# Sliding-window attention on one core: scores in quarters of the TensorE array, then used as weights over rows of values, gated values and ones

## The chip, the cores and the metric

The kernel runs on one core of a Trainium2 chip. A core has TensorE (PE, matmuls; its weight loads are shown apart as PEld), VectorE (DVE), ScalarE (ACT), GpSimd (POOL) and SyncE (SP), each with an instruction queue of its own, and 16 DMA engines that all queues share. The metric is the device time of one execution in microseconds (us). Everything is float32.

## The reference

Attention with a causal window of 64 keys over 8 batches, 8 heads, 576 positions and head size 64; its output, 512 wide for each of the 4608 tokens, goes into a mixture of 8 experts. A token takes its own best expert or that of the token before it, as a local gate says.

```python
scores = scale * np.matmul(q, k.transpose(0, 1, 3, 2))
rel = pos[:, None] - pos[None, :]
mask = (rel >= 0) & (rel < window)            # window = 64
...
attn = attn / (np.sum(attn, axis=-1, keepdims=True) + 1e-09)
x = np.matmul(attn, v)                         # then (B, S, H*D)
...
logits = np.einsum('bsd,de->bse', x, w_gate)
local_gate = 1.0 / (1.0 + np.exp(-np.einsum('bsd,de->bse', x, w_local).squeeze(-1)))
...
            e = fresh_e if s == 0 or local_gate[b, s] < 0.5 else prev_e
            h = np.maximum(x[b, s] @ w1[e], 0.0)
            out[b, s] = p[e] * (h @ w2[e])
```

## The kernel before

The program has three stages: `attention`, which writes the attended rows to `xs` in DRAM and the nine gate sums of each token (8 experts and the local gate) to `lt`; `route`, which sorts tokens by expert; and `experts`, which gathers the rows and runs the two matmuls of each expert. A `flag` behind attention says whether the sums of exponentials were in a safe range (line 110 writes `bad`); if not, a careful version would run, which it doesn't on these inputs. The routing's instructions stand behind the flag.

Attention runs over 9 chunks of 512 tokens (`sc`), and in each over 4 pairs of heads (`hp`). One pair of heads of one chunk is a unit. Keys and queries come in blocks of 64, and a query block needs its own key block and the one before. The steps of a unit:

- `scores` (lines 170 to 185): for each of 8 key blocks one matmul whose weights, `kt`, are a 128x128 block-diagonal matrix made on the host: the first head's 64 keys in one corner, the second head's in the other, zeros elsewhere. It is multiplied with 128 queries (the block itself and the next). The result, keys in rows, goes to `sp`; ScalarE makes exponentials of it (line 183, 1024 wide), VectorE multiplies with the mask (line 184).
- `values` (lines 187 to 206): the same with block-diagonal values `vt`, nine matmuls that leave `xp`, features in rows, tokens in columns (one of them takes the last key block of the chunk before). GpSimd adds up the exponentials that belong to one query into `t` (lines 199 to 204), and ScalarE copies `xp` to `xt`.

Once a chunk, `gates` multiplies `xt` with the gate weights and `t` with a selector of ones: eight matmuls of 512 columns, each 32 outputs wide in one of four column strips of the array. `rows` turns the gate sums (4 transposes) and `xt` (16 transposes) back to tokens in rows, divides by the sums (`r`), adds up the gates into `lt`, and stores 128 rows at a time to `xs` through GpSimd's queue (line 244). The two buffers of `x` come free when such a store has landed. `load` brings `qt` (1152 KB), `kt` and `vt` (2048 KB each) for a chunk through SP's queue, two chunks ahead at the start, one chunk ahead later. The order of instructions on all engines is the scheduler's.

Of the kernel before, what the change touches and what calls it, by code (L numbers as in the profile page):

```python
# [8 lines left out]
F32 = mybir.dt.float32  # L9
# [9 lines left out]
P = 128  # L19
# [4 lines left out]
WIN = 64  # L24
# [22 lines left out]
GW = 32  # L47


@with_exitstack  # L50
def kernel(
# [5 lines left out]
    k2: bass.AP,  # L57
    v2: bass.AP,
# [28 lines left out]
    attention(tc, q, k2, v2, xs, lt, ok, wg2s, ident)  # L87
# [26 lines left out]
def attention(ctx, tc, q, k2, v2, xs, lt, ok, wg2, ident):  # L114
# [22 lines left out]
    col = cp.tile([P, 2 * KB, WIN], I32, name="col")  # L137
    nc.gpsimd.iota(col, pattern=[[0, 2 * KB], [1, WIN]], base=0, channel_multiplier=0)
    colf = cp.tile([P, 2 * KB, WIN], F32, name="colf")
    nc.vector.tensor_copy(colf, col)  # L140
    mask = cp.tile([P, 2 * KB, 2 * WIN], F32, name="mask")
    nc.vector.tensor_scalar(mask[:, :, :WIN], colf, rowf, None, Alu.is_ge)
    nc.vector.tensor_scalar(mask[:, :, WIN:], colf, rowf, None, Alu.is_lt)
    nc.vector.memset(mask[:, KB - 1, WIN:], 0.0)


    sel = cp.tile([P, GW], F32, name="sel")
    nc.vector.memset(sel, 0.0)
    for i in range(2):
        nc.vector.memset(sel[i * WIN:(i + 1) * WIN, 2 * (E + 1) + i:2 * (E + 1) + i + 1], 1.0)  # L150

    allsum = cp.tile([P, NSC, 4, H], F32, name="allsum")

    qts, kts, vts = {}, {}, {}

    def load(sc):
        t0 = sc * SC
        n = min(SC + WIN, N - t0)
        qt = qts[sc] = qp.tile([P, HP, SC + WIN], F32, name="qt")
        kt = kts[sc] = qp.tile([P, HP, KB, P], F32, name="kt")  # L160
        vt = vts[sc] = qp.tile([P, HP, KB, P], F32, name="vt", bufs=3)
        step = 1 if sc == 0 else HP
        for i in range(0, HP, step):
            h = slice(i, i + step)
            nc.sync.dma_start(out=qt[:, h, :n], in_=q[:, h, t0:t0 + n])
            nc.sync.dma_start(out=kt[:, h], in_=k2[sc, :, h])
            nc.sync.dma_start(out=vt[:, h], in_=v2[sc, :, h])

    last = {}

    def scores(sc, hp):
        qt, kt = qts[sc], kts[sc]
        sp = ps_s.tile([P, KB, 2 * WIN], F32, name="sp")
        for j in range(KB):
            n = 2 * WIN if sc * KB + j + 1 < N // WIN else WIN
            nc.tensor.matmul(sp[:, j, :n], lhsT=kt[:, hp, j, :],  # L176
                             rhs=qt[:, hp, j * WIN:j * WIN + n], start=True, stop=True)
        p = pp.tile([P, KB, 2 * WIN], F32, name="p")
        m = (KB - sc if sc else KB)
        full = KB if (sc + 1) * SC < N else KB - 1  # L180
        for a, b, w in ((0, full, 2 * WIN), (full, KB, WIN)):
            if a < b:
                nc.scalar.activation(p[:, a:b, :w], sp[:, a:b, :w], Act.Exp, scale=DH ** -0.5)  # L183
                nc.vector.tensor_tensor(p[:, a:b, :w], p[:, a:b, :w], mask[:, m + a:m + b, :w], op=Alu.mult)  # L184
        return p

    def values(sc, hp, p, t, xt):
        vt = vts[sc]
        before = last.get(hp)
        xp = ps_x.tile([P, SC], F32, name="xp")  # L190
        if before is not None:
            nc.tensor.matmul(xp[:, :WIN], lhsT=vts[sc - 1][:, hp, KB - 1, :], rhs=before[:, KB - 1, WIN:],
                             start=True, stop=False, skip_group_check=True)
        for j in range(KB):
            n = 2 * WIN if j + 1 < KB else WIN
            nc.tensor.matmul(xp[:, j * WIN:j * WIN + n], lhsT=vt[:, hp, j, :], rhs=p[:, j, :n],  # L196
                             start=(before is None and j == 0), stop=(j == KB - 1), skip_group_check=True)

        nc.gpsimd.tensor_tensor(t[:, hp, WIN:].rearrange("p (b q) -> p b q", q=WIN), p[:, 1:, :WIN],  # L199
                                p[:, :KB - 1, WIN:], op=Alu.add)  # L200
        if before is not None:
            nc.gpsimd.tensor_tensor(t[:, hp, :WIN], p[:, 0, :WIN], before[:, KB - 1, WIN:], op=Alu.add)
        else:
            nc.gpsimd.tensor_copy(t[:, hp, :WIN], p[:, 0, :WIN])
        nc.scalar.copy(xt[:, hp, :], xp)
        last[hp] = p

    def gates(sc, t, xt):

        gp = ps_x.tile([P, SC], F32, name="gp")  # L210
        for hp in range(HP):
            g = gp[hp * GW:(hp + 1) * GW, :]
            nc.tensor.matmul(g, lhsT=wg2[:, hp, :], rhs=xt[:, hp, :], start=True, stop=False, skip_group_check=True)
        for hp in range(HP):
            g = gp[hp * GW:(hp + 1) * GW, :]
            nc.tensor.matmul(g, lhsT=sel, rhs=t[:, hp, :], start=False, stop=True, skip_group_check=True)
        gs = wk.tile([P, SC], F32, name="gs")
        nc.vector.tensor_copy(gs, gp)
        return gs

    def rows(sc, xt, gs):
        gt = ps_x.tile([P, 4, HP, GW], F32, name="gt")
        for c in range(4):
            nc.tensor.transpose(gt[:, c].rearrange("p h g -> p (h g)"), gs[:, c * P:(c + 1) * P], ident)
        su = allsum[:, sc].rearrange("p c (h j) -> p c h j", j=2)
        nc.vector.tensor_copy(su, gt[:, :, :, 2 * (E + 1):2 * (E + 1) + 2])
        r = wk.tile([P, 4, H], F32, name="r")
        nc.vector.tensor_scalar(r, allsum[:, sc], 1e-9, None, Alu.add)
        nc.vector.reciprocal(r, r)
        for c in range(4):  # L230
            n = sc * 4 + c
            g = wk.tile([P, HP, 2, E + 1], F32, name="g")
            rc = r[:, c, :]
            nc.vector.tensor_tensor(g, gt[:, c, :, :2 * (E + 1)].rearrange("p h (j e) -> p h j e", j=2),
                                    rc.rearrange("p (h j o) -> p h j o", j=2, o=1).to_broadcast([P, HP, 2, E + 1]),
                                    op=Alu.mult)
            nc.vector.tensor_reduce(lt[:, n, :], g.rearrange("p h j e -> p e (h j)"), axis=AX.X, op=Alu.add)
            xr = ps_x.tile([P, H, DH], F32, name="xr")
            for hp in range(HP):
                nc.tensor.transpose(xr[:, 2 * hp:2 * hp + 2, :].rearrange("p h d -> p (h d)"),  # L240
                                    xt[:, hp, c * P:(c + 1) * P], ident)
# [9 lines left out]
    for i, (sc, hp) in enumerate(units):  # L251
        if hp == 0:
            t = wk.tile([P, HP, SC], F32, name="t")
            xt = wk.tile([P, HP, SC], F32, name="xt")
# [515 lines left out]
```

## Time and profile before

| what | us |
|---|---|
| median of 3 runs (883.41 to 887.78) | 885.82 |
| the profiled execution | 886.19 |
| its span, first to last instruction | 883.9 |
| TensorE busy in the span | 802.9 |
| VectorE busy | 194.2 |
| ScalarE busy | 110.8 |
| GpSimd busy | 163.5 |

The page divides the span into 40 equal slices of 22.1 us. The windows, the timeline, the waits and the groups of instructions are answers from the same trace for a stretch or an engine. In a line of the timeline stand the start, the duration, the engine, the line of the program, the operation, what is written and read, the shapes, the count of merged instructions, and in brackets how long the engine had been idle and who released it. A float32 matmul shows as two MATMUL and two LDWEIGHTS instructions (two passes), a transpose as one of each.

### The profile page before, as it was taken

Reading aid. Unit: us, or ns where it says so; the run is one execution under the profiler, and the core shown is the slowest. Engines: PE = TensorE matmul, PEld = TensorE weight load, DVE = VectorE, ACT = ScalarE, POOL = GpSimd, SP = SyncE. Lnnn points to the kernel's source line nnn. Section 1 sums busy time; section 2 is a strip of 40 time slices with the busy share of each in tenths; the row PEclk is TensorE's granted clock in tenths of the full one; section 3 lists DMA queues with packets and bytes.
Section 4 is the critical chain, followed back from the end, with each engine's and each line's share of the span. In section 5 each row is a group of like instructions: output and inputs, shape, how many; then the busy total and the mean of one; then the engine's idle time right before and its main releaser. Section 6 shows DMA issues by size and latency. Waiting matters only on the chain. (4 is left out here: it accounts for less than half of the span.)

```text
span 883.9 us, 10273 instructions
## 1 busy us (share of the span) xinstructions
PE 802.9 (91%) x4279; PEld 596.2 (67%) x4279; DVE 194.2 (22%) x468; ACT 110.8 (13%) x158; POOL 163.5 (18%) x209
## 2 busy tenths in 40 slices
PE   6998888989455599999999999999999999999996
PEld 6787687878143367766676667766777777676864
DVE  3443444454794010000110011000101010101010
ACT  2232222222000000100001000100000101010100
POOL 2433332343102200111110111111111111111000
PEclk9999899899655599999999999999999999999999
DMA  9967766541104995354544545364888888888883
GB/s 342 411 274 292 293 253 237 210 199 67 47 0 187 420 403 202 125 232 147 216 166 185 207 162 217 132 234 144 318 328 328 322 323 324 329 329 318 313 305 122
DMA packets 27147, 213.50 MB, mean 242 GB/s; under 512 B 3821, under 2 KB 3837, under 8 KB 16848
## 3 DMA queue, kind: packets, MB, share of 16 engines
q1 hardware_dynamic: 17472, 182.46, 53.6%
q0 software_dynamic: 9616, 30.24, 8.7%
q8 instruction: 38, 0.62, 0.3%
q14 instruction: 21, 0.17, 0.1%
HBM read 193.81 MB, written 19.92 MB: 242 GB/s over the span
## 5 line engine op out<-in xcount | busy, mean ns | idle before, releaser
L686 PEld LDWEIGHTS hp<-xt,w 128*128 128x128 f32 x1856 | 266.6, 192 | 31.6 <-issue 13.4
L686 PE MATMUL hp<-xt,w 128*128 128x128 f32 (+1 forms) x1856 | 287.2, 316 | 0.0
L698 PE MATMUL yp<-w,h 128*128 128x512 f32 x640 | 279.5, 592 | 0.0
L698 PEld LDWEIGHTS yp<-w,h 128*128 128x128 f32 x640 | 119.5, 190 | 139.3 <-issue 137.0
L690 DVE TENSOR_SCALAR h<-hp 128x512 f32<-128x512 f32 x40 | 27.7, 692 | 522.7 <-issue 401.3
L702 POOL DMA_INDIRECT out_dram<-y,idx x40 | 40.0, 999 | 304.7 <-ACT y L701 291.6
L196 PE MATMUL xp<-p,vt 128*128 128x128 f32 (+1 forms) x576 | 77.6, 290 | 15.8 <-DVE p L184 15.6
L660 POOL DMA_INDIRECT xg<-xs,idx x43 | 42.1, 979 | 258.4 <-PE tp L674 191.4
L196 PEld LDWEIGHTS xp<-p,vt 128*128 128x128 f32 x576 | 73.6, 206 | 17.5 <-DVE p L184 16.3
L176 PE MATMUL sp<-qt,kt 128*128 128x128 f32 x576 | 78.3, 289 | 7.5 <-DMA kt<-in_k_dram 7.5
L176 PEld LDWEIGHTS sp<-qt,kt 128*128 128x128 f32 x576 | 72.6, 202 | 13.7 <-issue 13.7
L701 ACT ACTIVATE y<-yp,pw 128x512 f32<-128x512 f32 x40 | 27.5, 687 | 367.6 <-PE yp L698 357.8
L199 POOL TENSOR_TENSOR t<-p 128x448 f32<-128x448 f32 x36 | 44.9, 1248 | 68.9 <-DVE p L184 68.9
L184 DVE TENSOR_TENSOR p<-p,mask 128x1024 f32<-128x1024 f32 (+2 forms) x40 | 45.0, 1141 | 44.6 <-ACT p L183 44.6
L692 ACT ACTIVATE h<-hp 128x512 f32<-128x512 f32 x40 | 23.9, 597 | 224.1 <-PE hp L686 224.1
L183 ACT ACTIVATE p<-sp 128x1024 f32<-128x1024 f32 (+2 forms) x40 | 36.9, 933 | 91.4 <-PE sp L176 71.3
L674 PE MATMUL tp<-ident,xg 128*128 128x128 f32 x160 | 25.7, 296 | 21.8 <-DMA xg<-xs,idx 21.8
L674 PEld LDWEIGHTS tp<-ident,xg 128*128 128x128 f32 x160 | 20.3, 153 | 24.8 <-issue 21.0
L243 DVE TENSOR_TENSOR x<-xr,r 128x512 f32<-128x512 f32 x36 | 24.7, 685 | 42.2 <-DMA xs<-x 41.2
L244 POOL DMA_DIRECT2D xs<-x x36 | 19.7, 548 | 71.6 <-DVE x L243 37.8
L633 PE MATMUL tab<-colh,rowh 128*128 128x86 f32 x72 | 22.4, 467 | 10.7 <-DVE colh L632 10.7
L240 PE MATMUL xr<-ident,xt 128*128 128x128 f32 x144 | 23.4, 284 | 8.4 <-DVE x L243 8.4
(152 smaller groups left out, 270.9 us busy)
## 6 DMA issues: line engine op xcount, KB each, us to landing
w<-in_w_dram SPq DMA_DIRECT2D x64, 2048.0 KB, 8.2
kt<-in_k_dram SPq DMA_DIRECT2D x8, 2048.0 KB, 11.9
vt<-in_v_dram SPq DMA_DIRECT2D x8, 2048.0 KB, 13.7
xs<-x POOLq DMA_DIRECT2D x36, 256.0 KB, 3.8
qt<-in_q_dram SPq DMA_DIRECT2D x7, 1152.0 KB, 6.3
kt<-in_k_dram SPq DMA_DIRECT2D x4, 512.0 KB, 8.8
vt<-in_v_dram SPq DMA_DIRECT2D x4, 512.0 KB, 9.5
qt<-in_q_dram SPq DMA_DIRECT2D x4, 288.0 KB, 8.1
```

The lines of the kernel that those rows point to most:

```text
L176: nc.tensor.matmul(sp[:, j, :n], lhsT=kt[:, hp, j, :], rhs=qt[:, hp, j * WIN:j * WIN + n], start=True, stop=True)
L183: nc.scalar.activation(p[:, a:b, :w], sp[:, a:b, :w], Act.Exp, scale=DH ** -0.5)
L184: nc.vector.tensor_tensor(p[:, a:b, :w], p[:, a:b, :w], mask[:, m + a:m + b, :w], op=Alu.mult)
L196: nc.tensor.matmul(xp[:, j * WIN:j * WIN + n], lhsT=vt[:, hp, j, :], rhs=p[:, j, :n], start=(before is None and j == 0), stop=(j == KB - 1 ...
L199: nc.gpsimd.tensor_tensor(t[:, hp, WIN:].rearrange("p (b q) -> p b q", q=WIN), p[:, 1:, :WIN], p[:, :KB - 1, WIN:], op=Alu.add)
L660: nc.gpsimd.indirect_dma_start(out=x, out_offset=None, in_=xs[:, :], in_offset=bass.IndirectOffsetOnAxis(ap=idx[:, s:s + 1], axis=0))
L674: nc.tensor.transpose(tp[:, kk, :], x[:, kk * P:(kk + 1) * P], ident)
L686: nc.tensor.matmul(hp[:, i, :], lhsT=st["w1"][:, kk, m * P:(m + 1) * P], rhs=st["xt"][:, kk, :n], start=(kk == 0), stop=(kk == DK - 1))
L690: nc.vector.tensor_relu(o, hp)
L698: nc.tensor.matmul(yp, lhsT=st["h"][:, m, i * P:(i + 1) * P], rhs=st["w2"][:, m, :], start=(m == 0), stop=(m == FK - 1))
L701: nc.scalar.activation(y, yp, Act.Copy, scale=pw[:, s:s + 1])
L702: nc.gpsimd.indirect_dma_start(out=out[:, :], out_offset=bass.IndirectOffsetOnAxis(ap=idx[:, s:s + 1], axis=0), in_=y, in_offset=None, bou ...
```

## The change

The block-diagonal matrices go. Instead, `load` brings keys, queries and values with features in rows as they are (`kt`, `qt`, `vtt`, 1024 KB each), and values with tokens in rows, `va`, where each head's 64 values are followed by nine places for gate values and a one (74 wide).

- A score matmul takes the 64 keys of one head as weights. Head `j` of the pair stands in partitions 64 `j`, and key blocks of even number write partitions 0 to 63 of `sp`, those of odd number 64 to 127. So the four matmuls that follow each other stand in the four quarters of the array. There are 18 in a unit.
- `gates` multiplies the values themselves (`vtt`) with the gate weights, before attention instead of behind it: four matmuls of 512 columns a chunk. `spread` transposes the result (4 transposes) and puts it into the places of `va`. GpSimd then copies `va` into `vb`, whose second 64 rows are shifted by one pair of key blocks (lines 201 to 206).
- A value matmul takes the masked exponentials of 64 queries as weights, 128 keys deep, and multiplies the 74 columns of `va` (odd query blocks) or `vb` (even ones). So values, gates and the sum of exponentials come out of one matmul with tokens in rows: 16 in a unit, in two column strips, and no transposes of `xt`. VectorE takes the reciprocal of the sums and multiplies gates (`g`) and values (`x`) with it.
- A chunk is stored with one DMA, and its gates are reduced with one instruction.
- Buffers: four of `kt`, three of `qt` and `va`, two of `vtt` and `vb`, four of `p`; in PSUM two of `sp` and two of `xo`, two banks each. TensorE's order is that of the program (`manual_schedule`); scores run two units ahead of values (`LEAD`).

```diff
+VW = DH + E + 2
+LEAD = 2
+MID = (KB, KB - 1)
...
-    pp = ctx.enter_context(tc.tile_pool(name="at_p", bufs=HP + 3))
+    kp = ctx.enter_context(tc.tile_pool(name="at_k", bufs=3))
+    pp = ctx.enter_context(tc.tile_pool(name="at_p", bufs=LEAD + 2))
...
-    ps_x = ctx.enter_context(tc.tile_pool(name="at_ps_x", bufs=1, space=PSUM))
+    ps_x = ctx.enter_context(tc.tile_pool(name="at_ps_x", bufs=2, space=PSUM))
+    ctx.enter_context(tc.manual_schedule(engines={ET.PE}))
...
+        vtt = vts[sc] = qp.tile([P, HP, SC], F32, name="vtt")
+        kt = kts[sc] = kp.tile([P, HP, SC], F32, name="kt", bufs=4)
+        qt = qts[sc] = qp.tile([P, HP, SC], F32, name="qt", bufs=3)
+        va = vas[sc] = kp.tile([P, 4, H, VW], F32, name="va")
+        nc.sync.dma_start(out=vtt, in_=vt[:, :, t])
...
+            nc.sync.dma_start(out=kt[:, h], in_=k[:, h, t])
+            nc.sync.dma_start(out=qt[:, h], in_=q[:, h, t])
+        nc.sync.dma_start(out=va, in_=v3[t].rearrange("(c p) h x -> p c h x", p=P))
...
+    def gates(sc):
+
+        vtt = vts[sc]
+        r = ps_x.tile([P, 2, SC], F32, name="xo")
+        for hp in range(HP):
+            nc.tensor.matmul(r[hp * GW:(hp + 1) * GW, 0, :], lhsT=wg2[:, hp, :], rhs=vtt[:, hp, :],
+                             start=True, stop=True)
+        gs = wk.tile([P, SC], F32, name="gs")
+        nc.scalar.copy(gs, r[:, 0, :])
+        return r, gs
+
+    def spread(sc, r, gs):
+
+        va = vas[sc]
+        for c in range(4):
+            nc.tensor.transpose(r[:, 1, c * P:(c + 1) * P], gs[:, c * P:(c + 1) * P], ident)
+        nc.vector.tensor_copy(va[:, :, :, DH:DH + E + 1],
+                              r[:, 1, :].rearrange("p (c h g) -> p c h g", c=4, h=H)[:, :, :, :E + 1])
+        vb = vbs[sc] = kp.tile([P, 4, H, VW], F32, name="vb", bufs=2)
+        nc.gpsimd.tensor_copy(vb[:WIN], va[:WIN])
+        nc.gpsimd.tensor_copy(vb[WIN:, 1:], va[WIN:, :3])
+        if sc:
+            nc.gpsimd.tensor_copy(vb[WIN:, 0], vas[sc - 1][WIN:, 3])
...
     def scores(sc, hp):
         qt, kt = qts[sc], kts[sc]
-        sp = ps_s.tile([P, KB, 2 * WIN], F32, name="sp")
-        for j in range(KB):
-            n = 2 * WIN if sc * KB + j + 1 < N // WIN else WIN
-            nc.tensor.matmul(sp[:, j, :n], lhsT=kt[:, hp, j, :],
-                             rhs=qt[:, hp, j * WIN:j * WIN + n], start=True, stop=True)
...
+        sp = ps_s.tile([P, 2, SC], F32, name="sp")
+
+        def one(j, c, kt, block, a, b):
+            h = slice(j * DH, (j + 1) * DH)
+            nc.tensor.matmul(sp[c * WIN:(c + 1) * WIN, j, a:b], lhsT=kt[h, hp, block * WIN:(block + 1) * WIN],
+                             rhs=qt[h, hp, a:b], start=True, stop=True)
+
+        for s in range(5):
+            for c in range(2):
+                for j in range(2):
+                    if c == 0:
+                        if s < 4:
+                            one(j, 0, kt, 2 * s, s * P, (s + 1) * P)
+                    elif s:
+                        one(j, 1, kt, 2 * s - 1, s * P - WIN, min(s * P + WIN, SC))
+                    elif sc:
+                        one(j, 1, kts[sc - 1], KB - 1, 0, WIN)
+                    else:
+                        one(j, 1, kt, 1, 0, WIN)
+        p = pp.tile([P, 2, SC], F32, name="p")
+        nc.scalar.activation(p, sp, Act.Exp, scale=DH ** -0.5)
...
+        nc.vector.tensor_tensor(p, p, m.to_broadcast([P, 2, SC]), op=Alu.mult)
...
+    def values(sc, hp, p, x, g):
+        va, vb = vas[sc], vbs[sc]
+        xo = ps_x.tile([P, 2, SC], F32, name="xo")
+        for s in range(4):
+            for j in range(2):
+                for par, w in enumerate((vb, va)):
+                    b = 2 * s + par
+                    nc.tensor.matmul(xo[par * WIN:(par + 1) * WIN, j, s * VW:(s + 1) * VW],
+                                     lhsT=p[:, j, b * WIN:(b + 1) * WIN], rhs=w[:, s, 2 * hp + j, :],
+                                     start=True, stop=True)
+        o = xo[:, :, :4 * VW].rearrange("p j (c x) -> p j c x", x=VW)
+        r = allr[:, sc, hp]
+        nc.vector.reciprocal(r, o[:, :, :, VW - 1])
...
+            if sc + 2 < NSC:
+                load(sc + 2)
+        if i + LEAD < len(units):
+            ps[units[i + LEAD]] = scores(*units[i + LEAD])
+        if gated:
+            spread(sc + 1, *gated)
+            gated = None
+        values(sc, hp, ps.pop((sc, hp)), x, g)
+        if hp == 0 and sc + 1 < NSC:
+            gated = gates(sc + 1)
         if hp == HP - 1:
-            done = sc, t, xt
...
+            nc.gpsimd.dma_start(out=xs[sc * SC:(sc + 1) * SC, :].rearrange("(c p) d -> p c d", p=P),
+                                in_=x.rearrange("p c h j d -> p c (h j d)"))
```

How TensorE's queue stands in the middle of attention, first before: a unit's scores and values, and the chunk's gate matmuls.

```order
L176 MATMUL sp<-qt,kt 128x128 x8
L192 MATMUL xp<-p,vt 128x64
L196 MATMUL xp<-p,vt 128x128 x7
L196 MATMUL xp<-p,vt 128x64
L213 MATMUL gp<-xt,wg2s 32x512 x4
L216 MATMUL gp<-t,sel 32x512 x4
```

And TensorE's queue now, at the place in a chunk where the next chunk's gates are made (`xo` is the PSUM tile of the gates, of their transposes and of the values).

```order
L187 MATMUL xo<-vtt,wg2s 32x512 x4
L214 MATMUL sp<-qt,kt 64x128 x2
L214 MATMUL sp<-qt,kt 64x64 x2
L214 MATMUL sp<-qt,kt 64x128 x12
L214 MATMUL sp<-qt,kt 64x64 x2
L197 MATMUL xo<-ident,gs 128x128 x4
L243 MATMUL xo<-vb,p 64x74
L243 MATMUL xo<-va,p 64x74
```

The gate matmuls have moved from behind a chunk's values to a chunk ahead of them, and the pair of value rows stands eight times in a unit; scores of 128 outputs have become scores of 64.

VectorE's queue in the middle of attention before: masks between the steps of `rows` of the chunk before.

```order
L184 TENSOR_TENSOR p<-p,mask 128x1024 x2
L218 COPY gs<-gp 128x512
L184 TENSOR_TENSOR p<-p,mask 128x1024
L226 COPY allsum<-gt 128x32
L228 TENSOR_SCALAR r<-allsum 128x32
L229 RECIPROCAL r<-r 128x32
L234 TENSOR_TENSOR g<-gt,r 128x72
L243 TENSOR_TENSOR x<-xr,r 128x512
L237 TENSOR_REDUCE lt<-g 128x9
```

And VectorE's queue now, around the end of a chunk and the spread of the next one's gates.

```order
L275 TENSOR_REDUCE lt<-g 128x36
L233 TENSOR_TENSOR p<-p,mask_138 128x1024
L248 RECIPROCAL allr<-xo 128x8
L250 TENSOR_TENSOR g<-xo,allr 128x2x4x9
L252 TENSOR_TENSOR x<-xo,allr 128x2x4x64
L198 COPY va<-xo 128x32x9
```

The products `x` now stand in the unit whose values they take, and the copy of the gates goes into `va`, where GpSimd's copies and the next chunk's value matmuls wait for it.

## Rows read from the trace of the kernel before

**Rows 1.** The page, 40 slices: granted TensorE clock and DMA share, in tenths.

```profile
PEclk9999899899655599999999999999999999999999
DMA  9967766541104995354544545364888888888883
```

**Rows 2.** The timeline: first and last VectorE step of the flag (six steps).

```profile
224.69 0.30 DVE L271 TENSOR_SCALAR f<-allsum 128x288 f32<-128x288 f32 x1
...
228.98 0.14 DVE L110 TENSOR_SCALAR bad<-lo 1x1 int32<-1x1 f32 x1
```

**Rows 3.** Windows by chunk: busy us (instructions) of each engine, clock, DMA share, GB/s.

```profile
135.10:161.70 26.60, 22.21 (x173) 19.62 (x173) 10.80 (x20) 6.44 (x8) 8.57 (x12) 0.87 0.61 243
...
186.00:206.10 20.10, 19.58 (x174) 17.88 (x174) 11.01 (x23) 6.46 (x10) 7.78 (x12) 1.00 0.14 53
```

**Rows 4.** Waits in 35 to 222 us: total us, times, longest.

```profile
DVE x L243 <- DMA xs<-x: 41.2, 8, 8.0
```

**Rows 5.** The timeline of one stall, and the window of TensorE's work behind it.

```profile
153.37 0.69 DVE L243 TENSOR_TENSOR x<-xr,r 128x512 f32<-128x512 f32 x1 [7.68 <-DMA xs<-x]
...
155.25 3.68 PE L196 MATMUL xp<-p,vt 128*128 128x128 f32 x16 [3.86 <-DVE p L184]
155.35 1.97 POOL L199 TENSOR_TENSOR t<-p 128x448 f32<-128x448 f32 x1 [0.45 <-DVE p L184]
...
155.30:158.80 3.50, 3.50 (x16) 3.44 (x16) 1.03 (x1) 0.00 (x0) 3.45 (x4) 0.50 0.99 421
```

**Rows 6.** The timeline of TensorE: gate matmuls, then full-array passes.

```profile
158.85 0.20 PEld L213 LDWEIGHTS gp<-xt,wg2s 128*32 128x32 f32 x8
...
160.55 1.03 PE L216 MATMUL gp<-t,sel 128*32 128x512 f32 x8
...
161.52 2.05 PE L176 MATMUL sp<-qt,kt 128*128 128x128 f32 x16
...
163.41 0.33 PE L192 MATMUL xp<-p,vt 128*128 128x64 f32 x2
...
163.57 1.95 PE L196 MATMUL xp<-p,vt 128*128 128x128 f32 x16
...
165.36 0.61 PE L224 MATMUL gt<-ident,gs 128*128 128x128 f32 x4
...
166.24 1.73 PE L176 MATMUL sp<-qt,kt 128*128 128x128 f32 x14
```

**Rows 7.** VectorE groups by shape, 35 to 222 us; then the routing's reduction.

```profile
L184 DVE TENSOR_TENSOR p<-p,mask 128x1024 f32<-128x1024 f32 x28 | 35.1, 1268 | 24.6 <-ACT p L183 24.6
L243 DVE TENSOR_TENSOR x<-xr,r 128x512 f32<-128x512 f32 x31 | 21.3, 686 | 42.1 <-DMA xs<-x 41.2 <-PE xr L240 0.9
...
L234 DVE TENSOR_TENSOR g<-gt,r 128x72 f32<-128x72 f32 x31 | 6.3, 226 | 0.2
...
231.77 0.45 DVE L483 TENSOR_REDUCE mx<-lt 128x36 f32<-128x288 f32 x1
```

**Rows 8.** ScalarE groups by shape, 35 to 222 us: the exponentials.

```profile
L183 ACT ACTIVATE p<-sp 128x1024 f32<-128x1024 f32 x28 | 28.7, 1024 | 68.8 <-PE sp L176 48.7 <-DVE g L234 19.4 <-issue 0.7
```

**Rows 9.** GpSimd: an iota, then min/median/max ns of the sums `t`.

```profile
3.66 1.09 POOL L138 IOTA col<- 128x1024 int32 x1
...
L199 POOL TENSOR_TENSOR t<-p x36: 1121/1131/1976, 11.8 to 217.2; 128x448 f32<-128x448 f32 x36
...
L204 POOL COPY t<-p x4: 228/235/237, 12.9 to 27.1; 128x64 f32<-128x64 f32 x4
```

**Rows 10.** Two windows, and the load of the gate weights, its issue and landing.

```profile
0.00:25.00 25.00, 17.37 (x110) 16.95 (x111) 7.10 (x14) 6.46 (x7) 7.59 (x17) 1.00 0.94 350
...
5.70:35.00 29.30, 26.83 (x172) 22.85 (x173) 8.59 (x14) 6.35 (x8) 5.23 (x8) 1.00 1.03 405
...
L85 POOL DMA_DIRECT2D wg2s<-in_wg_dram x1: 598/598/598, 3.0 to 3.0; - x1
...
DMA to landing us min/median/max: 7.1/7.1/7.1
```

More of the change, by code (lines that the diff above doesn't have):

```diff
@@ L56 @@
     v: bass.AP,
-    k2: bass.AP,
-    v2: bass.AP,
+    v3: bass.AP,
+    vt: bass.AP,
     wg: bass.AP,
@@ L85 @@
     nc.gpsimd.dma_start(out=wg2s, in_=wg2)
-    attention(tc, q, k2, v2, xs, lt, ok, wg2s, ident)
+    attention(tc, q, k, v3, vt, xs, lt, ok, wg2s, ident)
     bad = const.tile([1, 1], I32, name="bad")
@@ L113, in attention @@
 @with_exitstack
-def attention(ctx, tc, q, k2, v2, xs, lt, ok, wg2, ident):
+def attention(ctx, tc, q, k, v3, vt, xs, lt, ok, wg2, ident):
     nc = tc.nc
@@ L142, in attention @@
[L142 to L148, printed above, removed]
-    for i in range(2):
[L150 to L167, printed above, removed]
@@ L169, in attention @@
-    last = {}
+    masks = []
+    for i in range(2):
+        m = cp.tile([P, KB, 2, WIN], F32, name=f"mask{i}")
+        for c in range(2):
+            h = slice(c * WIN, (c + 1) * WIN)
+            for par in range(2):
+                nc.vector.tensor_scalar(m[h, :, par, :], colf[h], rowf[h], None, Alu.is_ge if par == c else Alu.is_lt)
+        mid = MID[i]
+        other = slice((1 - mid % 2) * WIN, (2 - mid % 2) * WIN)
+        nc.vector.memset(m[other, mid // 2, mid % 2, :], 0.0)
+        masks.append(m.rearrange("p a b q -> p (a b q)"))
@@ L181, in scores @@
[L181 to L184, printed above, removed]
-        return p
[L187 to L241, printed above, removed]
-            x = wk.tile([P, H, DH], F32, name="x")
-            nc.vector.tensor_tensor(x, xr, rc.rearrange("p (h o) -> p h o", o=1).to_broadcast([P, H, DH]), op=Alu.mult)
-            nc.gpsimd.dma_start(out=xs[n * P:(n + 1) * P, :], in_=x.rearrange("p h d -> p (h d)"))
@@ L248, in attention @@
+    gated = gates(0)
+    spread(0, *gated)
     units = [(sc, hp) for sc in range(NSC) for hp in range(HP)]
-    ps = {units[0]: scores(*units[0])}
-    done = None
+    ps = {u: scores(*u) for u in units[:LEAD]}
+    gated = None
     for i, (sc, hp) in enumerate(units):
         if hp == 0:
-            t = wk.tile([P, HP, SC], F32, name="t")
-            xt = wk.tile([P, HP, SC], F32, name="xt")
-        if i + 1 < len(units):
-            ps[units[i + 1]] = scores(*units[i + 1])
-        values(sc, hp, ps.pop((sc, hp)), t, xt)
-        if hp == 0 and 1 <= sc < NSC - 1:
-            load(sc + 1)
-        if hp == 1 and done:
-            rows(*done)
-        if hp == 0 and done:
-            done = done[0], done[2], gates(*done)
-        if hp == HP - 1:
-            done = sc, t, xt
```

57 lines of the change are left out of this document (35 added, 22 removed).

## The prediction

> **What bounds the kernel now.** Read the page's 40 slices first [rows 1]: of 884 us, the first ten slices are attention, the next three the routing, the rest the experts. The change touches attention alone. Its last instruction is the flag, which ends at 229.1 us [rows 2]; the routing's own tables are made behind it. Everything from there on, some 655 us, has the same instructions before and after, so the whole question is at what time that flag ends.
>
> Next, the windows between one chunk's copy of the gate sums and the next (eight of them) [rows 3]. In 135.1:161.7 a chunk of 512 tokens takes 26.6 us while later chunks load (243 GB/s), with TensorE busy for 22.2 of them in 173 passes (a float32 matmul shows as two passes, a transpose as one). In 186.0:206.1, where nothing is loaded any more (53 GB/s), 174 passes take 20.1 us, 19.6 of them busy. So TensorE is the bound, and loading adds some 6 us a chunk. The waits say how [rows 4]: VectorE stood 8 times, 41.2 us in all, before `x` until an earlier store of `xs` had landed. [...] Over the chunk the granted clock is 0.87; where nothing loads it is 1.00 [rows 3]. Two costs, then: 20 us of matmuls a chunk, and the stores that queue behind 2 MB loads.
>
> **TensorE after the change.** A full-array pass over 128 columns costs 0.11 us in a row: 14 took 1.73 us and 4 took 0.61, each with one drain [rows 6]. A matmul is two of them. Before, a unit (one head pair of one chunk) has 8 score and 9 value matmuls, and a chunk also eight 512-column gate matmuls and 20 transposes: 4 x 34 + 16 + 20 = 172 passes, the 173 or 174 that the windows count.
> After, a unit has 18 score matmuls (14 of 128 columns, 4 of 64), each in one quarter of the array. If the four quarters run beside each other, each streams 512 columns twice: 8 x 0.11 = 0.88 us. That column strips do so is in the trace: the four gate matmuls on `sel`, eight passes of 512 columns, took 1.03 us [rows 6], what two passes need in a row. That row halves do so too no row shows; if not, it is 1.75 us. The 16 value matmuls (74 columns, two strips of 64 outputs) are 32 passes of 74/128 x 0.11 = 0.064 us, by twos: 1.02 us. Two changes of array shape a unit: I take 0.12 us each, from the last `sel` matmul (two passes of 512 columns from 160.55, 8 x 0.11 = 0.88 us, end at 161.43) to the next score pass at 161.52 [rows 6], rounded up. A unit is 0.88 + 1.02 + 0.24 = 2.1 us; a chunk with its gates (1.03) and four transposes (0.5) with their switches about 10.4 us, or 14 us if row halves don't overlap.
> The unseen price is that of issuing: 4 x 68 + 8 + 4 = 284 passes a chunk, each with its own weight load, against 172. The trace has eight weight loads of 32 columns inside 0.20 us [rows 6] and two passes of 64 columns with their loads within 0.33 us, drain included, but in a long row nothing faster than 0.11 us a pass, and there streaming explains it. Between those bounds I take under 50 ns, 14 us a chunk, nearer to the burst, since four such passes and their loads do start together.
>
> **VectorE and ScalarE.** A unit's mask product stays 1024 wide, 1.27 us; `x` stays 512 wide from PSUM, 0.69; the gate product of 72 is 0.23; the reciprocal of 8 sums from PSUM is bounded by that same 0.23 [rows 7]. That is 2.4 us a unit, 9.6 a chunk. The spread copy and the reduction over a whole chunk, 288 elements each, go at 0.45 (the reduction of 288 that the routing makes) [rows 7]: 10.5 us a chunk, what it is now. Four small products and four reductions are gone, one copy of 512 is gone. ScalarE has 4 exponentials of 1.02 [rows 8] and the gate copy: 5 us. Both lie beneath what follows.
>
> **GpSimd.** Instead of the sums `t`, three copies build `vb`, one block later for odd rows: 2368 + 1776 + 592 = 4736 elements a partition. A GpSimd copy of 64 took 0.235 us, an `iota` of 1024 took 1.09 (1.06 ns an element, fixed part included), the two-input product 1.13 for 448 (2.5 ns) [rows 9]. A copy reads one input, so I take the iota's rate, 5.0 us, and 0.5 for three starts; 11.9 us is the other end. Beside a VectorE mask the same product took 1.97 instead of 1.13 [rows 5], so two masks met add 1.7: 7.2 us. These copies stand between the spread of chunk n+1, in unit 1 of chunk n, and the first value matmul of chunk n+1, three units later; the cycle through them is 7.2 plus some 4 us (value, gate and score matmuls, ScalarE's copy, the transposes), 11 us, below the transfers. Its store of `xs` is one a chunk, queued behind the copies, and a buffer of `x` has a whole chunk to drain before it is wanted: the 41.2 us of [rows 4] go.
>
> **Transfers.** A chunk now loads 3 x 1024 KB (`vt`, `k`, `q`) and 128 x 4 x 8 x 74 x 4 B = 1184 KB (`va`): 4.36 MB, and stores 1.05 MB; before it loaded 5.37. The loads are independent of what went before by one to two chunks (four buffers of `kt`, three of `qt` and `va`), so the queue need not run dry. Its rate when full: 350 GB/s in the first 25 us, at 0.94 share, and 405 over 5.7:35.0 [rows 10], where half the bytes come in long rows. All rows are now 2 to 2.4 KB, so I take 355. That is 5.41/0.355 = 15.2 us a chunk, over TensorE's 10.4 to 14, VectorE's 10.5 and GpSimd's 11. **The transfers become the bound.**
>
> **The sum.** Up to the last `va` nine chunks are loaded and seven stored: 39.2 + 7.3 = 46.6 MB, 131 us at 355 GB/s; with 3 us to start, 134.2. The masks (ten small VectorE instructions where there were three) are made while the first loads are on the way, and SP issues four loads a chunk for three. That the first matmul now needs `wg2s`, which lands at 3.0 + 7.1 = 10.1 us [rows 10], lies beneath the 12 us that the first chunk's loads take. After the last `va`: spread 0.5, copies 7.2, four units by VectorE 9.6, the reduction 0.45, the six steps of the flag (from the first comparison of 0.30 to the last of 0.14) [rows 2] with hand-overs 2.4. The flag ends at 154.4 us, 74.7 earlier. The profiled execution took 886.2 (its span 883.9 and 2.3 around it); 886.2 - 74.7 = 811.5, and the median of the runs lies 0.4 lower: **811 us**. At 405 GB/s and with copies of 5 us it is 792 to 794; at 350 with a lost 0.5 us a chunk for the clock (TensorE idles a few us a chunk, as it does now) some 818.
>
> **Rivals.** *Issue is the bound, moderately.* At 55 to 70 ns a pass a chunk takes 15.6 to 19.9 us. With the first value matmul at 20 us (load, gates, copies) and 3 at the end, the flag ends at 163 to 202: 820 to 859. For it: 65% more passes, and none of the trace runs on at such a rate; against it: the bursts. [...]
> [...]
> *The quarters run one after another.* Scores are then 3.4 us a unit, a chunk 4 x (3.4 + 1.0 + 0.24) + 1.8 = 20.4: the flag at 207, 864 us. The strips of [rows 6] speak against it. *GpSimd's copies decide.* At 11.9 us and four masks met the cycle is 19 us: the flag at 194, 851 us.
>
> **How the numbers follow.** Transfers bound (792 to 820): 0.58. Moderate issue bound: 0.17. Copies: 0.10, mostly at 820 to 850. Serial quarters: 0.05. Issue at about 81 ns: 0.03, and above: 0.07. Faster by over 0.5% (what a measurement of this kernel can tell): 0.90; same 0.03; slower 0.07. The range runs from 793 (faster transfers, shorter copies) to 860, which leaves out the last 0.10, most of the serial case and a little on either side, some 0.18.
>
> **What would show it.** In the windows by chunk: 15 us each, DMA share near 0.95 to 1.0 from the start to 130 us, some 350 GB/s, and the flag near 154. TensorE's busy time 9 to 11 us a chunk. The waits: VectorE's spread copy waits for `va`, TensorE's gates for `vtt`. If instead DMA share is about 0.8 and TensorE starts its short passes at an even 60 ns or more with nothing to wait for, it is issue; if four score passes don't start together, the quarters; if the value matmuls wait for `vb`, the copies. A rate below 330 GB/s with the queue full would make the transfer step wrong.

## The result, and the profile after

The changed kernel takes 798.5 us (median of 4 runs, 797.36 to 799.42) against 885.34 for the kernel before on the same chip: a ratio of 0.9017, 95% interval 0.8991 to 0.9044. A second set of five runs gave 798.72 and 0.900 (0.8979 to 0.902). The profiled execution took 797.36 us, its span is 795.6. Forecast were 811 us and a range of 793 to 860.

The end of attention moved as the page's slices show (granted clock and DMA share, in tenths; answers to [rows 1]): DMA is full in the first six slices of 19.9 us, and attention ends in the eighth; before, attention filled ten slices of 22.1 us.

```profile
PEclk9999999555599999999999999999999999999998
DMA  9999993104995544536455364468888888889883
```

The flag, on VectorE's timeline (start, duration, engine, line, operation; answers to [rows 2]), ends at 143.12 us. It ended at 229.12, and 154.4 was forecast. What follows takes 652.4 us, for 654.8 before; in the run e8_start below, with the same instructions behind the flag, 654.4. So these 2 us are no work of the change.

```profile
140.93 0.30 DVE L283 TENSOR_SCALAR f<-allr 128x288 f32<-128x288 f32 x1
...
142.98 0.14 DVE L113 TENSOR_SCALAR bad<-lo 1x1 int32<-1x1 f32 x1
```

The windows by chunk, from one chunk's reduction to the next (length, then busy us and instructions of PE, PEld, DVE, ACT, POOL, then clock, DMA share, GB/s; answers to [rows 3]):

```profile
64.40:79.00 14.60, 11.61 (x293) 9.52 (x295) 10.36 (x18) 4.16 (x5) 6.17 (x5) 1.00 1.04 397
79.00:92.70 13.70, 11.14 (x295) 9.34 (x292) 10.65 (x18) 4.77 (x6) 6.17 (x5) 1.00 1.04 397
...
107.50:121.30 13.80, 10.28 (x269) 8.55 (x263) 9.94 (x19) 4.68 (x5) 8.01 (x5) 1.00 0.88 339
```

A chunk takes 13.3 to 14.8 us, DMA is full at 395 to 397 GB/s, and TensorE is busy for only 10 to 12 us of it. This looks like the forecast's "transfers become the bound". But the waits in 26 to 120 us (engine, tile and line, what it waited for: us in all, times, longest; answers to [rows 4]) hold no wait for a load or a store at all:

```profile
ACT p L230 <- PE sp L214: 40.4, 23, 3.1
POOL vb L201 <- DVE va L198: 31.6, 7, 6.8
DVE p L233 <- ACT p L230: 14.8, 14, 3.8
...
PE xo L243 <- issue: 7.8, 6, 1.8
PE sp L214 <- issue: 7.8, 7, 1.5
DVE va L198 <- PE xo L197: 7.6, 5, 2.2
...
PE xo L187 <- issue: 1.1, 1, 1.1
...
PE xo L187 <- PE xo L243: 0.4, 1, 0.4
```

VectorE waits for ScalarE, ScalarE for TensorE, and TensorE stands still waiting for nothing that the profile shows ("issue"). Its timeline shows where (answers to [rows 6]):

```profile
61.55 1.12 PE L214 MATMUL sp<-qt,kt 64*64 64x128 f32 x36
...
62.90 0.23 PE L243 MATMUL xo<-vb,p 128*64 128x74 f32 x1
64.89 0.28 PE L243 MATMUL xo<-vb,p 128*64 128x74 f32 x1 [1.76 <-issue]
...
66.81 1.12 PE L214 MATMUL sp<-qt,kt 64*64 64x128 f32 x36
67.86 0.66 PE L197 MATMUL xo<-ident,gs 128*128 128x128 f32 x4
```

36 score passes take 1.05 us from their start to that of what follows (66.81 to 67.86): 29 ns each, so all four quarters run beside each other. But in the middle of a unit's value matmuls, between two passes that need the same data, TensorE stops for 1.8 us. The list of waits counts 14 such holes from 26 to 120 us, 16.7 us in all: six among value matmuls, seven among scores, one among gate matmuls. Only one other wait of TensorE stands beside them (0.4 us). They come by count and not by place: from one to the next the trace has 126 to 128 passes, each time.

Each has a counterpart among the transfers. Queue q8, which the page calls "instruction", moves pieces of 16 KB; one is under way in the microsecond from 62 to 63, just before that hole. Here are its line for that microsecond, then lines for the whole stretch 26 to 110 us (packets, MB, share of the DMA engines):

```profile
q8 instruction: 1, 0.02, 6.5%
...
DMA packets 14812, 33.15 MB, mean 395 GB/s; under 512 B 485, under 2 KB 485, under 8 KB 14797
q1 hardware_dynamic: 13437, 27.68, 87.6%
...
q8 instruction: 13, 0.21, 1.0%
```

That piece runs from 62.30 to 63.34, and TensorE goes on at 64.89. So it is with all 14: TensorE resumes 1.3 to 1.6 us behind a piece's landing. Up to the flag there are 2557 passes and 20 pieces, 128 passes a piece; before, 1537 and 12, again 128. A pass shows as two instructions, a weight load and a matmul (5295 of each on the page), so a piece goes with 256 of them. From 30.7 to 106.8 us, the pieces start 6.2 to 6.7 us apart, evenly, 6.3 in the mean: 49 ns a pass. Before, they were 14 to 21 us apart, and in the same stretch there were five:

```profile
q8 instruction: 5, 0.08, 0.4%
```

A chunk of the new kernel has 284 passes, 2.22 pieces, 14.0 us at that distance. Its transfers, 5.41 MB at 395 GB/s, take 13.7. Both are what a chunk takes (14.0 in the mean of the six up to 121.3), so this profile can't tell which of them sets it. The experiments do.

Last, the groups of VectorE and GpSimd on the page (count, busy us, mean ns, idle before; answers to [rows 7] and [rows 9]): the mask takes 1.47 us in the mean for 1.27, and a copy to `vb` of 2368 elements 3.0 us, 1.27 ns an element.

```profile
L233 DVE TENSOR_TENSOR p<-p,mask 128x1024 f32<-128x1024 f32 x36 | 52.6, 1466 | 15.4 <-ACT p L230 15.4
...
L201 POOL COPY vb<-va 64x2368 f32<-64x2368 f32 x9 | 27.0, 2999 | 45.9 <-DVE va L198 45.9
```

### The profile page after: what moved, and what is told of

Same layout as the page of the kernel before. It is cut to its first block, busy times and chain, and to the rows that moved or that the text cites. A ratio compares the mean times of both kernels' runs of the same rounds, so it can differ in the third digit from the quotient of the medians.

```text
span 795.6 us, 12193 instructions
## 1 busy us (share of the span) xinstructions
PE 710.3 (89%) x5295; PEld 509.8 (64%) x5295; DVE 194.3 (24%) x450; ACT 95.3 (12%) x127; POOL 153.3 (19%) x137
## 5 line engine op out<-in xcount | busy, mean ns | idle before, releaser
L243 PE MATMUL xo<-vb,p 128*64 128x74 f32 x576 | 47.2, 233 | 12.1 <-issue 6.1
L233 DVE TENSOR_TENSOR p<-p,mask 128x1024 f32<-128x1024 f32 x36 | 52.6, 1466 | 15.4 <-ACT p L230 15.4
L214 PE MATMUL sp<-qt,kt 64*64 64x128 f32 (+1 forms) x1296 | 45.6, 278 | 7.8 <-issue 7.8
L243 PEld LDWEIGHTS xo<-vb,p 128*64 128x64 f32 x576 | 40.6, 138 | 15.3 <-issue 8.3
L214 PEld LDWEIGHTS sp<-qt,kt 64*64 64x64 f32 x1296 | 39.3, 143 | 17.3 <-issue 15.3
L243 PE MATMUL xo<-va,p 128*64 128x74 f32 x576 | 47.3, 233 | 2.7 <-issue 2.7
L230 ACT ACTIVATE p<-sp 128x1024 f32<-128x1024 f32 x36 | 36.9, 1025 | 61.6 <-PE sp L214 50.7
L243 PEld LDWEIGHTS xo<-va,p 128*64 128x64 f32 x576 | 40.6, 138 | 4.1 <-issue 4.1
L201 POOL COPY vb<-va 64x2368 f32<-64x2368 f32 x9 | 27.0, 2999 | 45.9 <-DVE va L198 45.9
L687 DVE COPY xt<-tp 128x512 f32<-128x512 f32 x40 | 26.5, 681 | 19.1 <-PE tp L686 19.1
```

What stands on the lines that cost most here:

```text
L201: nc.gpsimd.tensor_copy(vb[:WIN], va[:WIN])
L214: nc.tensor.matmul(sp[c * WIN:(c + 1) * WIN, j, a:b], lhsT=kt[h, hp, block * WIN:(block + 1) * WIN], rhs=qt[h, hp, a:b], start=True, stop= ...
L230: nc.scalar.activation(p, sp, Act.Exp, scale=DH ** -0.5)
L233: nc.vector.tensor_tensor(p, p, m.to_broadcast([P, 2, SC]), op=Alu.mult)
L243: nc.tensor.matmul(xo[par * WIN:(par + 1) * WIN, j, s * VW:(s + 1) * VW], lhsT=p[:, j, b * WIN:(b + 1) * WIN], rhs=w[:, s, 2 * hp + j, :], ...
```

## The experiments

The theory: TensorE's instruction stream, a 16 KB piece each 6.3 us while loads fill the DMA engines, is a bound of its own beside the transfers. The rivals: transfers alone, GpSimd's copies, the streaming of columns on TensorE. Where a kernel computes something else, tokens go to other experts and the time behind the flag changes, so there the flags are compared. Each flag is of one execution; the changed kernel's two lie 1.1 us apart (143.1, and 144.2 in its second profile, after_again).

**What the stores were worth: e6_before_six_x.** The kernel before, with one edit:

```diff
-            x = wk.tile([P, H, DH], F32, name="x")
+            x = wk.tile([P, H, DH], F32, name="x", bufs=6)
```

> The kernel before, with six buffers of x instead of two, so that VectorE need not wait for a store of xs to land (41.2 us in eight waits). If those waits held TensorE up, a chunk falls from 25 to 20 or 21 us, as in the chunk without loads: 855 us. Rival, another wait stands right behind: within 5 us of 885.

Measured: 859.36 us, ratio 0.9703 (0.9674 to 0.9732); the flag at 203.4, 25.8 earlier. VectorE's waits for stores are gone, and each chunk is now TensorE's:

```profile
100.00:120.00 20.00, 19.48 (x174) 17.79 (x173) 10.97 (x20) 6.44 (x8) 7.78 (x12) 1.00 0.82 320
```

Of the 86 us by which the change moves the flag, some 26 are the stores' waits, which four more buffers would have bought too. The other 60 come with the rest of the change, in which TensorE's busy time a chunk falls from 19.5 us to 10 to 12; how they divide between that and the smaller loads no run shows.

**Less to load: e1_less_load, e3_both; copies: e2_no_copies.** e1 keeps the queries of three chunks before from the fourth chunk on, e2 leaves `vb` as the first chunk made it, e3 does both.

```diff
-        qt = qts[sc] = qp.tile([P, HP, SC], F32, name="qt", bufs=3)
+        qt = qts[sc] = qts[sc - 3] if sc >= 3 else qp.tile([P, HP, SC], F32, name="qt", bufs=3)
...
-            nc.sync.dma_start(out=qt[:, h], in_=q[:, h, t])
+            if sc < 3:
+                nc.sync.dma_start(out=qt[:, h], in_=q[:, h, t])
```
```diff
-        vb = vbs[sc] = kp.tile([P, 4, H, VW], F32, name="vb", bufs=2)
+        if sc:
+            vbs[sc] = vbs[0]
+            return
+        vb = vbs[sc] = kp.tile([P, 4, H, VW], F32, name="vb", bufs=1)
```

> From the fourth chunk on, no queries are loaded (the first three chunks' stay in use, so the output is another): 6.3 MB less in six chunks, 15.9 us at 395 GB/s. Transfers bound the chunk (13.7 us): chunks 3 to 8 shorten to the next limit, some 12.4 us as in the one chunk of the changed kernel that no load accompanies, so the flag comes 8 us earlier, 790 us; 783 if nothing else limits above 11 us. Rival, the cycle spread - GpSimd's copies - value matmuls - gates - spread bounds the chunk: no change, 798 us, and the DMA share falls to 0.8.

> GpSimd copies vb for the first chunk alone and all chunks use that one (the output is another): 5.7 us of copies a chunk and their wait are gone. Transfers bound the chunk: it stays at 13.7 us while loads run, and only the way from the last load to the flag (22 us) loses one or two copies, 5 to 8 us: 791 us. Rival, the cycle through the copies bounds: the chunk falls by the 5.7 us to the transfers' or VectorE's time, below 11 us, 770 us or less.

> Both left out, the queries' loads from the fourth chunk on and the copies from the second on (the output is another). If transfers and the copies' cycle stand close one behind the other, this gains more than the two alone together: transfers need 11.0 us in chunks 3 to 8, VectorE 10.4, so the flag comes 16 us earlier by transfers and 6 at the end: 776 us. If TensorE with its holes in the middle of a unit (1.5 us each, two a chunk) bounds by itself, it stops near 12.4 us a chunk: 784 us.

Measured: e1 793.93 us, its flag at 137.8; e2's flag at 143.1, unchanged (842.79 us in all, the rest lying behind the flag); e3 793.27, flag 138.5. The copies cost nothing, at either load. The loads cost 5 us, not the 12 by which they end sooner (108.6 for 120.9). Two chunks of e1, one with loads and one with few:

```profile
78.30:91.20 12.90, 10.75 (x272) 8.95 (x270) 10.37 (x19) 4.20 (x6) 7.03 (x5) 0.96 0.85 297
...
105.00:117.10 12.10, 11.26 (x292) 9.18 (x284) 9.88 (x20) 4.69 (x5) 8.03 (x5) 1.00 0.38 151
```

In the first, the DMA engines are not full (0.85) and TensorE is busy for 10.75 us, and the chunk still takes 12.9: TensorE has a hole of 2.15 us in it, which ends 1.3 us behind a piece's landing. Transfers alone don't set it. The chunk between the two says less: it takes 13.8 us, but TensorE is busy for 13.18 of them, at a granted clock of 0.92.

**More to load: e4_more_load.** One more megabyte a chunk, into a buffer that nobody reads:

```diff
+        more = kp.tile([P, HP, SC], F32, name="more", bufs=2)
+        nc.sync.dma_start(out=more, in_=k[:, :, t])
```

> Each chunk loads another 1 MB into a tile that nobody reads: 9.4 MB more, 24 us at 395 GB/s. Transfers bound: 798 + 24 = 822 us, 16.4 us a chunk. Rival, they stood just beneath another bound of 13.4 us or so: the same from there on, some 2 us less. Rival, the queue had room: under 805 us.

Measured: 825.77 us, ratio 0.9333, the flag at 168.8. The last load lands at 146.7, 25.8 later, and the flag is 25.7 later: now transfers set the end, to the microsecond. TensorE's waits for issue are gone but for 1.9 us (26 to 120 us); it waits 14.9 us for the copies to `vb` instead. The megabytes added, 9.4, are 24 us at 395 GB/s, so the transfers had next to no slack in the changed kernel.

**Streaming: e5_head_by_head.** The same 18 score matmuls, one head behind the other, so that only two quarters work at a time:

```diff
-        for s in range(5):
-            for c in range(2):
-                for j in range(2):
+        for j in range(2):
+            for s in range(5):
+                for c in range(2):
```

> The same score matmuls, all of the pair's first head before all of the second, so that only the two column halves of one row half can run beside each other. The 36 passes of a unit take 1.8 to 1.9 us instead of 1.05. If TensorE is the bound, the nine chunks pay 36 x 0.8 = 29 us: 827 us; 815 if its holes (1.4 us, two a chunk) are shorter because passes are used up more slowly. If transfers alone bound and TensorE only waits for them, most of it is hidden: 798 to 804 us. If the halves never ran beside each other: no change at all in the 1.05 us.

Measured: 799.22 us, flag 144.1: no change beyond what two executions differ by. The scores do take 1.72 us for 1.12 (its timeline), which shows that the row halves ran beside each other in the changed kernel; but its waits for "issue" fall (in 26 to 110 us; the changed kernel has 7.8 and 6.1 there).

```profile
60.43 1.72 PE L214 MATMUL sp<-qt,kt 64*64 64x128 f32 x36
```
```profile
PE sp L214 <- issue: 1.2, 3, 0.6
PE xo L243 <- issue: 1.2, 2, 0.6
...
PE xo L187 <- issue: 0.2, 1, 0.2
```

The longer scores vanish into the holes: TensorE's waits for issue fall from 15.0 us to 2.6 there, while the pieces keep their 6.3 us. What TensorE does slower with the same instructions is paid for by the pause that it would have made anyway. So streaming is no bound. By the branches set down for it the run gives what transfers alone would give too (798 to 804); it doesn't part them from the instructions.

**More instructions: e7_scores_twice.** Each score matmul issued twice, 428 passes a chunk for 284:

```diff
-        for s in range(5):
+        for s in [0, 1, 2, 3, 4] * 2:
```

> Each score matmul is issued twice, the second overwriting the first with the same numbers: 144 passes more a chunk (428 for 284), same transfers. A 16 KB piece of the instruction stream is fetched for each 128 passes (a pass and its weight load are 128 bytes). If the holes in the middle of a unit come from these fetches, they rise from about two a chunk to over three, and the time by 36 x 1.05 + 9 x 1.1 x 1.4 = 52 us: 850 us. If the holes are anything else, two a chunk stay and it is 836 us. If transfers alone bound, TensorE has some 3 us a chunk to give: 810 us.

Measured: 832.96 us, flag 177.4. The time lies nearest to the branch for holes of another kind (836), and not to the one for pieces (850). But there are 3853 passes and 30 pieces up to the flag (128 each), and the waits for issue still go with them: from 26 to 121 us there are 11 (18.2 us), and each ends 1.2 to 1.5 us behind a piece's landing. The branch of 850 had wrong that every piece makes a hole: 16 pieces came there. Three chunks:

```profile
61.60:82.10 20.50, 18.15 (x468) 15.90 (x462) 10.48 (x18) 4.68 (x5) 6.18 (x5) 0.88 0.75 267
...
82.10:100.90 18.80, 15.52 (x463) 13.48 (x456) 10.73 (x18) 5.37 (x6) 7.02 (x5) 1.00 0.85 306
...
137.50:152.40 14.90, 14.90 (x454) 13.19 (x453) 10.70 (x18) 5.35 (x6) 7.05 (x5) 1.00 0.39 149
```

In the second, neither is DMA full (0.85) nor TensorE busy (15.5 of 18.8 us); in the first the granted clock is 0.88, and TensorE is busy for 18.15 of 20.5. With the loads nearly over, a chunk takes 14.9, all of it busy. 3.34 pieces at 6.3 us would be 21. The distance of the pieces goes with the loads, though not strictly: 6.0 to 6.5 us in the full stretch up to 56 us (DMA at 1.04 in 44 to 56), later four times 3.5 to 3.7, three of them with DMA at 0.75, 0.67 and 0.27 and one at 1.05, and three times about 4; then 3.3 to 4.8 when the loads are over.

**Half the scores, less to load: e11_less_load_half.** On top of e1, the second and fourth unit of a chunk take the scores of the one before:

```diff
-        sp = ps_s.tile([P, 2, SC], F32, name="sp")
+        if hp % 2 == 0:
+            held[0] = ps_s.tile([P, 2, SC], F32, name="sp")
+        sp = held[0]
...
-        for s in range(5):
+        for s in range(5 if hp % 2 == 0 else 0):
```

> No queries are loaded from the fourth chunk on, as in the first of these kernels, and the second and fourth unit of a chunk take the scores of the unit before (the output is another, and the time behind the flag may differ with the routing, so the flag is compared; it came at 137.8 us with the loads left out alone). TensorE streams 2.1 us less a chunk and fetches 0.56 pieces less, 0.8 us. If TensorE with its holes bounds that kernel, the flag comes at 124 to 128 us; if VectorE or ScalarE does, whose work is the same, at 135 or later.

Measured: 802.58 us, flag 147.2, later than e1's. Chunks take 13.1 to 13.8 us even where little loads (DMA at 0.22 to 0.26), at a granted clock of 0.87 to 0.89, and TensorE's value matmuls wait 20.4 us for VectorE (26 to 136 us), a wait that e1 doesn't have there. That two units sharing a tile of PSUM make these waits is likely but not shown. The run changed more than the number of passes and decides nothing.

**Fewer instructions for the same columns: e12_long_scores, e13_long_scores_less_load.** Eight score matmuls of 256 columns a unit for eighteen of 128 and 64; e13 has e1's edit as well.

```diff
-        for s in range(5):
+        for s in range(2):
...
-                    if c == 0:
-                        if s < 4:
-                            one(j, 0, kt, 2 * s, s * P, (s + 1) * P)
...
+                    one(j, c, kt, 4 * s + c, 2 * s * P, 2 * (s + 1) * P)
```

> The same score columns a quarter, but in 8 matmuls of 256 columns a unit instead of 18 of 128 and 64; a key block meets four query blocks instead of two, so scores and all that follows from them are others, and the tokens go to other experts: only the time up to the flag counts. Transfers, columns streamed, VectorE's, ScalarE's and GpSimd's work stay. A chunk has 204 passes for 284. If TensorE's instruction stream (a piece of 16 KB, 128 passes, each 6.3 us while loads run) is as near to the end as the transfers, TensorE's holes shrink from some 20 us to under 10 in 26:120, 1.6 pieces a chunk come where 2.2 came, and the chunks fall only to what the transfers take, 13.7 us for 13.9: the flag at 138 to 142 (after 143.1). If the number of passes has nothing to do with the holes, they stay at 20 us. If streaming is the bound, the chunks stay too.

> The long score matmuls and, besides, no loads of q from the fourth chunk on (the queries of three chunks before are taken); the output is another, and only the flag counts. Either one alone leaves one bound: less load left the flag at 137.8, with chunks of 12.9 to 14.5 us under loads. If that was held by the instruction stream, both together give what is next, 10.5 to 11.5 us a chunk (transfers 11.0, VectorE 10.5, TensorE's streaming 10.4, instructions 1.6 pieces x 6.3 = 10.0): the flag at 119 to 127. If the instruction stream is no bound, the flag stays at 136 to 139.

Measured: e12's flag at 140.0, e13's at 127.7; the scores take 1.09 us a unit on the timeline, for 1.12. e12's waits for a load and those of TensorE in 26 to 110 us, and its pieces there (9 for 13):

```profile
DVE va L198 <- DMA va<-in_v_dram: 12.7, 5, 5.3
...
PE xo L235 <- DVE va L198: 6.2, 4, 3.4
...
PE xo L187 <- issue: 5.5, 5, 1.1
```
```profile
q8 instruction: 9, 0.15, 0.7%
```

No wait for issue is left before a score or value matmul (13.9 us in the changed kernel). The five that are left stand before the gate matmuls of a chunk, 204 passes apart, and not behind a piece; the one at 60.37 us follows VectorE's last reading of a tile of `xo` (60.27), which may be what it waited for. VectorE waits for a load, which it never did in the changed kernel in this stretch, and TensorE waits for VectorE behind it. In all, TensorE stands still for nearly as long as before (13.7 us for 15.4), but for other things. The last load lands at 120.9, to the tenth where it did before: with fewer instructions the transfers are left, and only 3 us are won. Both together give 15.4 us, more than the 5.3 and 3.1 of either alone added up. Two chunks of e13, the first with the queue full, the second as the loads end:

```profile
71.50:82.90 11.40, 10.90 (x209) 7.19 (x204) 10.18 (x19) 4.68 (x5) 7.89 (x5) 1.00 1.04 399
...
95.80:107.10 11.30, 11.05 (x212) 7.28 (x204) 10.19 (x19) 4.68 (x5) 8.05 (x5) 1.00 0.64 248
```

11.4 us a chunk, at 1.04 of DMA as at 0.64: TensorE is busy for 10.9 of them, and the engines' own work is the bound at last. So two nearly equal bounds stand above it, and taking one away shows only the other. One chunk between these two takes 12.9 us, with a hole of 1.56 us that ends 1.3 us behind a piece's landing; the flag came 0.7 us past the upper end of what was expected (127).

**Another start: e8_start.** A complete version: the gate weights first on SP's queue, the first chunk's `va` behind its first pair, and that chunk's second copy on ScalarE.

```diff
-    nc.gpsimd.dma_start(out=wg2s, in_=wg2)
+    nc.sync.dma_start(out=wg2s, in_=wg2)
...
+            if sc == 0 and i == 0:
+                nc.sync.dma_start(out=va, in_=v3[t].rearrange("(c p) h x -> p c h x", p=P))
-        nc.sync.dma_start(out=va, in_=v3[t].rearrange("(c p) h x -> p c h x", p=P))
+        if sc:
+            nc.sync.dma_start(out=va, in_=v3[t].rearrange("(c p) h x -> p c h x", p=P))
...
-        nc.gpsimd.tensor_copy(vb[WIN:, 1:], va[WIN:, :3])
+        if sc:
+            nc.gpsimd.tensor_copy(vb[WIN:, 1:], va[WIN:, :3])
+        else:
+            nc.scalar.copy(vb[WIN:, 1:], va[WIN:, :3])
```

> The changed kernel with another start and nothing left out: the gate weights come first on SP's queue, the first chunk's values in rows are loaded right behind its first pair of keys and queries instead of last, and in that chunk alone ScalarE makes the second of the two copies into vb. The first value matmul, at 18.9 now (its last read copy ends at 21.4), should start at about 16.5; if all that follows moves along, the flag ends 3 to 5 us earlier, at 138 to 140, and the time is 794 to 796. If the load queue sets the end and not the chain of units (the same bytes are loaded, in another order), the flag stays within 1 us of 143.1 and the time at 798.

> The changed kernel once more, beside the others on the same chip: 798 to 800, its flag at 143 to 144 and pieces of 16 KB of instructions at 6.2 to 6.5 us from each other while loads run. If the distances of the pieces differ from those of the first profile, they belong to the chip or the execution and not to the program.

Measured: 798.05 us (796.71 to 799.44) beside 798.72 for the changed kernel on the same chip: no difference. The first value matmul does start 3 us sooner (15.91 for 18.87), and the first chunk ends sooner, but the third is level again. These are the reductions at the end of e8_start's first three chunks:

```profile
34.08 0.65 DVE L281 TENSOR_REDUCE lt<-g 128x36 f32<-128x288 f32 x1
48.80 0.67 DVE L281 TENSOR_REDUCE lt<-g 128x36 f32<-128x288 f32 x1
62.93 0.66 DVE L281 TENSOR_REDUCE lt<-g 128x36 f32<-128x288 f32 x1
```

The changed kernel's second profile has 35.68, 48.98 and 62.56. The same bytes are loaded, and the pieces come 6.3 us apart in the mean in both (6.0 to 6.8), so an earlier start is waited off. e1 and e5, each on another chip, have the same distance in the full stretch, so it belongs neither to a chip nor to one execution.

## Why the prediction was right, and where it was right for the wrong reason

**The bound before** stood as told. Taking the stores' waits away alone gave 25.8 us of flag and chunks of 20.0 us at 97% TensorE (e6), the 20 of [rows 3].

**TensorE's prices** held: 36 score passes 1.05 us to the next step for 0.88 and a switch of 0.12, 32 value passes 1.18 for 1.02 and the same switch (1.03 from the first start to the last), the four quarters beside each other (e5 shows what two cost). The rival of serial quarters falls.

**The transfers** were the mis-sized term. 355 GB/s was taken from near the 350 of the first 25 us; 395 to 397 were moved. The last `va` landed at 120.9 us for 134.2, 13.3 sooner; the steps behind it gave 2.0 back, and the flag came 11.3 us before its forecast. The higher row, 405, that [rows 10] also had, was the better one.

**The rest behind the last load** took 22.2 us for 20.2, through other steps. Spread and copies lay beneath the chunk before: when the last `va` landed, TensorE was finishing only the first unit of the chunk before the last, and seven more units followed at some 2.2 us each (the copies ended at 131.07, and the first value matmul that needs them stood in its turn at 131.27; without copies the flag stood still, e2). The rival of GpSimd's copies falls, and so do their 7.2 us in the sum. The copy itself was sized well: 3.0 and 2.3 to 2.5 us for the two that stand in the way, for 5.0 and a fixed part.

**Issue** is the step that failed in its reasoning. It was priced as a distance between passes, "under 50 ns, 14 us a chunk", and laid beneath the transfers' 15.2. Passes don't follow each other at 50 ns: scores run at 29 and values at 32. A price of that size is real all the same: a piece of instructions came for each 128 passes, and 128 passes each 6.3 us is 49 ns, 14.0 us a chunk. It goes with the loading beside it (3.3 to 4.8 us a piece when the loads are over, DMA at 0.39 and 0.22, in e7). And it is not hidden beneath the transfers, as the prediction had it, but stands level with them. The trace of before could have told the need (1537 passes, 12 pieces) but not the price: there no piece came sooner than 14 us behind another. The number came out by luck, and the sign given for it ("an even 60 ns or more") could not have shown it: the profile shows holes of 0.6 to 1.8 us in rows of quick passes. No run shows 81 ns as the price of issuing a pass, to which the forecast gives a chance of 0.03: in the changed kernel 36 passes in 1.05 us are 29 ns each, and over a whole chunk, holes included, 284 passes in 14.0 us are 49.

**"Transfers become the bound"** is half right. The waits named as its sign, VectorE's spread copy for `va` and the gates for `vtt`, don't stand in the changed kernel's profile from 26 to 120 us; the first of them comes up in e12. Transfers set when the last load lands (120.9 in e12 as in the changed kernel), and with a megabyte more a chunk they set all (e4). But with less to load most of the time stays (e1), with more instructions the time goes up while DMA has room (the second chunk shown of e7), and only both together open the next bound (e13). What sets the 6.3 us within the DMA engines is not shown; that it falls, to 3.3 to 4.8 us, when loads thin out is (e7).

## What to carry to other kernels

Count instructions as bytes: when a change replaces long matmuls by many short ones beside heavy loading, the time for 16 KB of instructions, here 128 weight loads and 128 matmuls in 6.3 us, is a term of the sum like any other, and the distance of the pieces in the instruction queue gives it, where the engine goes on just behind each piece (1.3 to 1.6 us here). Idle time of an engine with no releaser, in the middle of matmuls on the same data and each time behind the same number of passes (126 to 128), was the sign here; longer matmuls of the same total columns were the cure and the test (13.9 us of such waits before scores and values, none in e12). And where two bounds stand level, take both away in one run: either alone shows little (3 and 5 us here, and 15 together).

## What the runs showed of the hardware that was not expected

- Instruction pieces for TensorE came each 6.3 us with the DMA engines full (1.04) and each 3.3 to 4.8 us when the loads were over (DMA at 0.39 and 0.22, e7), and in the changed kernel TensorE went on 1.3 to 1.6 us behind a piece's landing.
- Sustained short passes go far below the 0.11 us that the kernel before showed: 29 ns for 64x128 in four quarters, 32 ns for 74 columns in two strips, 46 ns for scores in two quarters (1.65 us for 36, start to start).
- A VectorE mask and a GpSimd copy hold each other up, and the one that starts second pays. Behind the first 25 us of attention, the 11 masks that begin while a copy to `vb` runs take 1.4 to 2.1 us; all others take 1.2, also those during which a copy begins. A copy of 2368 elements that begins during a mask takes 3.1 us; the fastest, which doesn't, takes 2.15. Without the copies (e2) every mask from the second chunk on takes 1.2 us.
